# Linear attention into a phase-mixing MLP on one core: first q's by Pool's casting fetches, key-value products in runs of two, and a re-planned order

## The chip, the cores and the metric

The kernel runs on one core of a Trainium2 chip. The metric is the device time of the whole program in microseconds (us), here the median of several runs. The engines are PE (TensorE, the matrix array), DVE (VectorE), ACT (ScalarE), POOL (GpSimd) and SP (SyncE, which here only issues transfers).

## What is computed

Eight batches (B), eight heads (H), 576 positions (S), 64 columns a head (D); C = H·D = 512. Everything comes in and goes out as float32.

```python
kv  = einsum('bhsd,bhse->bhde', k, v)
out = einsum('bhsd,bhde->bhse', q, kv)
x   = out / sqrt(mean(out**2, -1) + 1e-6) * g_norm      # then heads side by side: [8, 576, 512]
theta = x @ w_theta
y   = w_tok_r @ (x * cos(theta)) + w_tok_i @ (x * sin(theta))   # over positions
u   = x + y
result = u + maximum(u @ w_ch, 0)
```

## The kernel before

A batch's 576 positions are worked on as four full tiles of 128 rows and a tail of 64. The functions inside the main function each describe one step of one batch `b`, and pair of heads `hp` or row tile `ti`:

- `load` (L402): q, k and v of a pair of heads, 256 or 288 KB each, fetched by SP. With `b < Q_SOFT`, q is fetched by Pool instead, as fp16 (L409), after a one-word copy of an earlier v tile on Pool (`hold`, L382, L385) that keeps Pool from running ahead. The tails of 64 rows are small fetches of their own; from batch 2 on, q's tail is fetched by Pool (L457). `hold` also keeps back the token mixers (L511, L516, until v number `MIX_AFTER`) and the channel weights (L544).
- `cast_q` (L598): DVE turns q into fp16 (L600). With `b < Q_SOFT` only the tail is cast (L606).
- `turn_q_pair` (L769): PE turns q of a pair, four 128-wide matmuls (L783), or with `b < Q_SOFT` eight, one for each head and row tile, into halves of the array's columns (L778); ACT or DVE copies the result into qT (L794, L796). `turn_q_tail` (L910) does the tail, and `double` (L744) copies its columns a second time so that the tail uses 128 columns. From batch 4 on, q is turned by a DMA (L626, L632).
- `attention` (L643): kv products in float32, in half of the array (L662); `KV_RUN` pairs stand in one task from batch 2 on. In batches 0 and 1 `by_pair` (L803) goes on pair by pair: raw product (L823), square (ACT, L830), sum (DVE, L836), root, scale (xp, L860), turn (xTps, L871), copy (xT, L882 and L884). Later batches do this by row tile in `norm` (L691) and `turn_x` (L934), where Pool takes the root (L721).
- `phase` (L986): theta product (PE, L996, L1001), its folding (pt on ACT, f and fa on DVE), two sines (tr on ACT, L1031, L1039), and z = x times both (DVE, L1049).
- `mix` (L1071): the token mixing y (PE, L1092), in six parts a batch; parts 0 and 1 of batch 0 are opened early and fed row tile by row tile. DVE forms uT (L1103).
- `channel` (L1125): u turned back by PE (ups, L1141) and copied by ACT (L1157), or, for batches from `U_FROM` up to the last, turned by a DMA (L1179); the product with w_ch (vps, L1150); the result (ot, DVE, L1161); its store.
- `idle_work` (L390): filler matmuls on PE that read nothing new (tile warm, L395).

None of these runs where it stands. Each is handed to `Weave.add` (L134) with the engines that could do it, a cost, a due time, the tasks that it needs and the buffers that it makes and uses. `Weave.run` (L145) then plans the order: it starts each engine at a time in `BEGIN`, keeps its own account of engines, transfers and buffers (`SLOTS`, L44), and on the engine that can begin first takes the task with the earliest due time. Due times are `START + PERIOD * b + first + every * i` from the table `DUE` (L21). `MARGIN`, `SLACK`, `URGENT`, `AHEAD` and `HOLD` shift its choices; `HOLD` is added where a task would change the array's form (whole array, halves, quarters). A filler is taken where PE has nothing else that can begin as early, up to the planned time `WARM`. The planned order is then fixed on each engine (`in_traced_order`, L246): on the chip every engine works through its list in that order, and waits at the head of it. The lists are thus known before the program runs, and both kernels' can be compared.

```python
def due(stage, b, i):
    (first, every) = DUE.get((stage, b), DUE[stage])
    return START + PERIOD * b + first + every * i
```

Of the kernel before, what the change touches and what calls it, by code (L numbers as in the profile page):

```python
# [15 lines left out]

PERIOD = 26.95
START = 4.0  # L20
DUE = {  # L21
    "load": (-21.61, 8.44),
    "theta": (0.39, 0),
    "mixers": (17.6, 0),
    "wch": (24.7, 1.25),
    "wT": (21.7, 1.67),
    ("phase", 0): (19.67, 0),
    ("mix", 0): (28.68, 4.96),
    ("channel", 0): (31.53, 7.53),
    ("phase", 1): (11.06, 3.64),  # L30
    ("mix", 1): (31.68, 5.24),
    ("channel", 1): (50.99, 7.88),
    ("first", 1): (-24.56, 1.26),
    "first": (0.46, 0),
    "cast": (27.66, 0.92),
    "turn_q": (-15.49, 0.49),
    "attention": (-2.51, 1.53),
    "norm": (-1.15, 4.11),
    "turn": (4.17, 1.73),
    "phase": (18.31, 3.76),  # L40
    "mix": (51.46, 2.87),
    "channel": (75.2, 4.3),
}
SLOTS = {  # L44
    "kv": 1, "raw": 2, "tp": 2, "th": 1, "mm": 3,
# [4 lines left out]
BANK = {"th": "mm", "y": "mm", "vp": "mm", "pu": "tp", "px": "tp"}  # L50
QUAD = 2
Q_DMA = 4
U_FROM = 2
X_FROM = 8
MIX_AFTER = 2
WCH_AFTER = 8
KV_RUN = 1
Q_SOFT = 0
QL_SOFT = 1


# [44 lines left out]
class Weave:  # L106
# [5 lines left out]

    SLACK = {"PE": 0.2, "ACT": 0.004, "DVE": 0.078, "POOL": 0.1, "SP": 0.05}
    MARGIN = {"PE": 0.247, "ACT": 0.026, "DVE": 0.555, "POOL": 0.1, "SP": 0.0}
    BEGIN = {"PE": 1.6, "ACT": 3.2, "DVE": 1.7, "POOL": 2.5, "SP": 0.73}
    WARM = 69.7
    COLD = 5.0
    URGENT = 5.5  # L120
    AHEAD = 0.3
    HOLD = 2.45
    DRAIN = 0.095
    ENTRY = {"F": 0.011, "R": 0.011, "H": 0.024, "K": 0.048, "Q": 0.048}
    ARRAY = {"F": 0, "R": 1, "H": 2, "K": 2, "Q": 3}
# [19 lines left out]
    def run(self):  # L145
# [25 lines left out]
        while ready:  # L171
            best = {}
            for t in ready:
# [8 lines left out]
                for (e, cost, lat, port) in engines:  # L182
                    new = e == "PE" and self.ARRAY[port] != form
                    clear = free[e] + self.DRAIN if new else free[e]
                    start = max(clear, at + self.MARGIN[e], port_free if port is True else 0.0)
                    if name[0] == "warm" and start > self.WARM:
                        continue
                    if due < self.URGENT:
                        start = max(clear, start - self.AHEAD)
                    best.setdefault(e, []).append(  # L190
                        (start, due + self.HOLD * new, max(at, port_free) if port is True else at, t, cost, lat, port)
                    )
            picks = []
            for (e, c) in best.items():
                first = min(x[0] for x in c) + self.SLACK[e]
                (start, due, at, t, cost, lat, port) = min(
# [66 lines left out]
def kernel(  # L263
# [45 lines left out]
    def sb(kind, shape, dtype, name):  # L309
        return work.tile(shape, dtype, tag=kind, bufs=SLOTS[kind], name=name)  # L310
# [53 lines left out]
    def dve(cost, fast=False):  # L364
        return ("DVE", cost, cost + 0.14, fast)

    def pe(cost, form="F"):
        return ("PE", cost, cost + 0.22, form)
# [13 lines left out]
    def hold(name, due, after):  # L382
        def fn(e):
            t = st[after]
            nc.gpsimd.tensor_copy(late[:], t[:, 0, 0:1] if len(t.shape) == 3 else t[:, 0, 0, 0:1])  # L385
        weave.add(name, [("POOL", 0.2, 0.22, False)], due, fn, needs=[after],
                  uses=["{}{}_{}".format(*after)])
# [14 lines left out]
    def load(b, hp):  # L402
        pair = slice(2 * hp, 2 * hp + 2)

        def part(kind, src):
            def fn(e):
                if kind == "q" and b < Q_SOFT:
                    t = sb("qh", [P, 2, NF, D], FP16, f"q{b}_{hp}")
                    nc.gpsimd.dma_start(  # L409
                        out=t[:].rearrange("p h j d -> p h (j d)"),  # L410
                        in_=src[b, pair, 0:SF, :].rearrange("h (p j) d -> p h (j d)", j=NF),
                    )
                elif kind == "q" or b >= QUAD:
                    t = sb(kind, [P, 2, NF, D], FP32, f"{kind}{b}_{hp}")
                    nc.sync.dma_start(
                        out=t[:].rearrange("p h j d -> p h (j d)"),
                        in_=src[b, pair, 0:SF, :].rearrange("h (p j) d -> p h (j d)", j=NF),
                    )
                else:
                    t = sb(kind, [P, NS, D], FP32, f"{kind}{b}_{hp}")  # L420
                    nc.sync.dma_start(
                        out=t[:].rearrange("p j d -> p (j d)"),
                        in_=src[b, pair].rearrange("h (p j) d -> (h p) (j d)", j=NS),
                    )
                st[kind, b, hp] = t
# [14 lines left out]
        for (i, (kind, src)) in enumerate((("q", q), ("k", k), ("v", v))):  # L440
            full = kind == "q" or b >= QUAD
            if kind == "q" and b < Q_SOFT:
                n = b * HP + hp
# [26 lines left out]
    def load_weights():  # L470
# [36 lines left out]
        use = due("mixers", 0, 0)  # L507
        hold("hold_mix", use, ("v", MIX_AFTER // HP, MIX_AFTER % HP))
        for (i, w) in enumerate((moe_w_tok_r, moe_w_tok_i)):
# [88 lines left out]
    def cast_q(b, hp):  # L598
# [8 lines left out]

        if hp == 0 and b < Q_SOFT:
            weave.add(("qcl", b), [dve(0.33, True)], due("first", b, hp) + (0.1 if b else 9.0), tail,
                      needs=[("ql", b)], makes=[("qc", f"qc{b}")], uses=[f"ql{b}"])  # L610
        if b < Q_SOFT:
            return
# [30 lines left out]
    def attention(b, hp):  # L643
        run = KV_RUN if b >= QUAD and b > 1 else 1

# [123 lines left out]
    def turn_q_pair(b, hp, at):  # L769
# [3 lines left out]
        def turn_q0(e):  # L773
            t = st[pq] = ps("tp", [P, SF], FP16, pq)
            for j in range(NF):
                if b < Q_SOFT:
                    for r in range(2):
# [10 lines left out]
        def keep_q0(e):  # L788
# [6 lines left out]
            else:  # L795
                nc.vector.tensor_copy(t, src)  # L796

        weave.add((pq,), [pe(0.226, "H" if b < Q_SOFT else "F")], at, turn_q0, needs=[("qc" if b >= Q_SOFT else "q", b, hp)], makes=[("tp", pq)],
                  uses=[f"qc{b}" if b >= Q_SOFT else f"q{b}_{hp}"])
# [325 lines left out]
    def channel(b, ti):  # L1125
# [5 lines left out]

        pu_on = not U_FROM <= b < B - 1 or ti == NF

# [71 lines left out]
# [4 lines that stand above are left out]
# [59 lines left out]
```

## Time and profile before

| | us |
|---|---|
| median of 3 runs | 214.65 (214.16 to 215.4) |
| the profiled execution | 215.4 |
| its span, first to last instruction | 213.6 |
| PE / DVE / ACT / POOL busy in the span | 203.7 / 177.3 / 150.5 / 89.6 |
| filler matmuls on PE (50) | 11.2 |
| y products (PE, L1092) | 78.1 |
| float32 kv products (PE, L662), k and v without tails | 27.1 |
| q casts on DVE (L600), 32 | 13.2 |
| theta product of batch 0 begins | 21.62 |

A timeline line gives the start, the duration, engine, source line, operation, output<-input with sizes, the number of instructions merged into it, and in brackets the idle time before it with what ended it. Matmuls overlap each other, so a matmul's own duration is longer than the step from one to the next, and a busy PE is not PE at its peak; where PE's work is counted here, it is by the step from start to start. A line of stretches gives the stretch and its length, then for PE, its weight loads, DVE, ACT and POOL the busy time with the number of instructions, the granted TensorE clock, the busy share of the DMA engines, and GB/s.

### The profile page before, as it was taken

To read this page: it belongs to the slowest core of one execution; us is meant where nothing else is said; L and a number is where in the kernel's file an instruction comes from. 1 tells how busy PE (TensorE), PEld (TensorE's weight loads), DVE (VectorE), ACT (ScalarE), POOL (GpSimd) and SP (SyncE) were. 2 spreads that over 40 slices of the span, in tenths; PEclk is the share of its full clock that TensorE was granted. 3 is DMA by queue.
4 is the path that set the end of the run, shared out by engine and by line. 5 is a ranking of instruction groups with operands and counts; after the bars stand their busy time and mean duration, and the time that the engine had idled before them with its cause. 6 is when DMAs were issued, how large, how long until landed. Compare 5 with 4: busy or idle time off the path is not lost.

```text
span 213.6 us, 5833 instructions
## 1 busy us (share of the span) xinstructions
PE 203.7 (95%) x2305; PEld 145.0 (68%) x2305; DVE 177.3 (83%) x355; ACT 150.5 (70%) x294; POOL 89.6 (42%) x104
## 2 busy tenths in 40 slices
PE   6897989999999999999999999999999999999992
PEld 4784567876488777677787577765777467568560
DVE  3178689877978889999999998999999989973652
ACT  2077699967984899898897859789688588550031
POOL 8050106595105763575474436574474733000000
PEclk9999999999999999999999999999999999999998
DMA  6999999999587599989898989859773263344424
GB/s 182 371 360 247 264 373 282 374 213 209 97 268 238 146 284 356 211 254 230 242 179 154 324 304 189 158 136 330 229 166 79 79 170 75 135 114 98 146 103 172
DMA packets 62463, 45.62 MB, mean 214 GB/s; under 512 B 33380, under 2 KB 55524, under 8 KB 62436
## 3 DMA queue, kind: packets, MB, share of 16 engines
q1 hardware_dynamic: 58272, 43.01, 70.7%
q0 software_dynamic: 4160, 2.25, 8.4%
q8 instruction: 18, 0.29, 0.6%
q14 instruction: 9, 0.07, 0.2%
q10 hardware_dynamic: 4, 0.00, 0.0%
HBM read 33.06 MB, written 9.44 MB: 199 GB/s over the span
## 4 chain that ended last, share of the span: by engine, by line
PE 62%; DVE 11%; DMA 8%; ACT 8%; POOL 6%; issue 2%; SPq 0%; DVEq 0%
PE y L1092 25%; PE vps L1150 12%; PE th L996 9%; PE kv L662 7%; DMA wch<-in_moe_w_ch_dram 4%; POOL rt L721 3%; DMA v<-in_v_dram 3%; PE xTps L943 2%; PE raw L699 2%; DVE ss L710 2%; POOL rt1h L855 2%; ACT tr L1031 2%; DMA k<-in_k_dram 2%; PE ups L1141 2%; DVE x L733 2%
## 5 line engine op out<-in xcount | busy, mean ns | idle before, releaser
L1092 PE MATMUL y<-wT,z 128*128 128x320 f16 (+1 forms) x576 | 78.1, 286 | 0.1
L1092 PEld LDWEIGHTS <-z 128*128 128x128 f16 x576 | 55.0, 98 | 16.2 <-issue 0.6
L721 POOL TENSOR_TENSOR rt<-ss,mhalf 128x8 f32<-128x8 f32 x31 | 56.5, 1822 | 2.6
L1150 PE MATMUL vps<-wch,uT 128*128 128x512 f16 (+1 forms) x192 | 36.5, 344 | 0.3 <-DMA wch<-in_moe_w_ch_dram 0.2
L1103 DVE SCALAR_TENSOR_TENSOR uT<-y,gcol,xT 128x320 f16<-128x320 f32 (+1 forms) x48 | 29.3, 613 | 6.9 <-PE y L1092 6.9
L1008 ACT ACTIVATE pt<-th,magic_t 128x512 f32<-128x512 f32 (+1 forms) x40 | 25.8, 645 | 9.1 <-PE th L996 5.6
L996 PE MATMUL th<-wth,xT 128*128 128x512 f16 x128 | 32.0, 379 | 0.0
L717 POOL TENSOR_SCALAR ss<-ss 128x8 f32<-128x8 f32 x31 | 8.4, 272 | 55.6 <-DVE ss L710 54.8
L662 PE MATMUL kv<-v,k 128*64 128x64 f32 (+1 forms) x672 | 27.1, 232 | 0.9 <-DMA v<-in_v_dram 0.9
L662 PEld LDWEIGHTS kv<-v,k 128*64 128x64 f32 (+1 forms) x672 | 24.3, 145 | 4.7 <-issue 3.6
L1012 DVE SCALAR_TENSOR_TENSOR f<-pt,th 128x512 f32<-128x512 f32 (+1 forms) x40 | 25.1, 628 | 2.5 <-ACT pt L1008 2.4
L1031 ACT ACTIVATE tr<-fa,pio_t 128x512 f16<-128x512 f32 x32 | 23.0, 720 | 1.8 <-DVE fa L1019 1.6
L1031 ACT ACTIVATE tr<-f 128x512 f16<-128x512 f32 x32 | 20.2, 630 | 5.6 <-DVE f L1012 5.4
L952 ACT ACTIVATE xT<-xTps,gcol 128x512 f16<-128x512 f16 (+1 forms) x32 | 20.1, 629 | 5.2 <-PE xTps L943 5.0
L733 DVE TENSOR_TENSOR x<-raw,rt 128x512 f16<-128x512 f32 x32 | 22.0, 686 | 2.1 <-POOL rt L721 1.6
L710 DVE TENSOR_REDUCE ss<-sq 128x8 f32<-128x512 f32 x32 | 21.8, 680 | 2.0 <-ACT sq L706 2.0
L1150 PEld LDWEIGHTS <-uT 128*128 128x128 f16 (+1 forms) x192 | 14.7, 102 | 11.7 <-issue 1.1
L1157 ACT COPY u<-ups 128x512 f16<-128x512 f16 (+1 forms) x20 | 9.9, 500 | 16.7 <-PE ups L1141 16.7
L1049 DVE TENSOR_TENSOR z<-x,tr 128x1024 f16<-128x1024 f16 (+1 forms) x32 | 19.7, 618 | 1.3 <-ACT tr L1039 0.9
L706 ACT ACTIVATE sq<-raw 128x512 f32<-128x512 f32 x32 | 19.0, 593 | 0.5 <-PE raw L699 0.5
L600 DVE CAST qcast<-q 128x512 f16<-128x512 f32 x32 | 13.2, 422 | 6.2 <-DMA q<-in_q_dram 6.2
L996 PEld LDWEIGHTS <-xT 128*128 128x128 f16 x128 | 11.5, 98 | 10.1 <-ACT xT L952 0.2
(105 smaller groups left out, 264.0 us busy)
## 6 DMA issues: line engine op xcount, KB each, us to landing
q<-in_q_dram SPq DMA_DIRECT2D x32, 256.0 KB, 5.0
out_dram<-ot SPq DMA_DIRECT2D x32, 256.0 KB, 3.0
k<-in_k_dram SPq DMA_DIRECT2D x24, 256.0 KB, 5.1
v<-in_v_dram SPq DMA_DIRECT2D x24, 256.0 KB, 4.9
k<-in_k_dram SPq DMA_DIRECT2D x8, 288.0 KB, 5.6
v<-in_v_dram SPq DMA_DIRECT2D x8, 288.0 KB, 5.5
wst<-in_moe_w_theta_dram SPq DMA_DIRECT2D x4, 256.0 KB, 5.8
out_dram<-ot SPq DMA_DIRECT2D x16, 64.0 KB, 2.1
```

Of the source, the lines that this page charges most:

```text
L662: nc.tensor.matmul(kvp[r * D:(r + 1) * D, hp, :], kt, vt, start=(j == 0), stop=(j == (NT if b >= QUAD else NS) - 1),)
L710: nc.vector.reduce_sum(out=t[:], in_=st[sq][:].rearrange("p (h e) -> p h e", h=H), axis=mybir.AxisListType.X,)
L721: nc.gpsimd.tensor_tensor(out=r[:], in0=t[:], in1=mhalf[:], op=ALU.pow)
L733: nc.vector.tensor_tensor(out=t[:].rearrange("p (h e) -> p h e", h=H), in0=st[raw][:].rearrange("p (h e) -> p h e", h=H), in1=st[rt][:].un ...
L952: nc.scalar.activation(out=st["xT", b][:, :, cols], in_=st[px][:, :, 0:cols.stop - cols.start], func=AFT.Copy, scale=gcol[:],)
L996: nc.tensor.matmul(t[:], xT[:, kc, :], wth[:, kc, :], start=(kc == 0), stop=(kc == NK - 1),)
L1008: nc.scalar.activation(out=t[:], in_=st[th][:], func=AFT.Identity, bias=magic_t[:])
L1012: nc.vector.scalar_tensor_tensor(out=t[:], in0=st[pt][:], scalar=MAGIC, in1=st[th][:], op0=ALU.subtract, op1=ALU.subtract,)
L1031: nc.scalar.activation(out=t[:, which, :], in_=src[:], func=AFT.Sin, scale=-RAD, bias=0.0 if bias is None else bias[:],)
L1092: nc.tensor.matmul(st[y][:, c, :], z[:, kc * P:(kc + 1) * P], wT[m][:, cols], start=(c == 0 and m == 0) if open_sums else m == 0, stop=m = ...
L1103: nc.vector.scalar_tensor_tensor(out=st["uT", b][:, chunks, cols], in0=st[y][:], scalar=gcol[:], in1=st["xT", b][:, chunks, cols], op0=ALU ...
L1150: nc.tensor.matmul(t[half], uT(kc), wch[:, kc, r * n:(r + 1) * n], start=(kc == 0), stop=(kc == NK - 1),)
```

## The change

Only constants change; the functions stay as they are.

- `Q_SOFT` 0 to 2: q of batches 0 and 1 is fetched as fp16 by Pool and turned per head in column halves; its cast on DVE goes (8 of 32).
- `KV_RUN` 1 to 2: from batch 2 on, the kv products of two pairs are one task.
- `U_FROM` 2 to 3: u of batch 2 is turned by PE and copied by ACT, not turned by DMAs.
- `MIX_AFTER` 2 to 4: the token mixers' fetch is held for the first v of batch 1, not for the third of batch 0.
- The due times, the period and the planner's margins change, and with them the order on every engine.

Counted in the fixed lists: fillers 50 to 63; turns of u on PE (L1141) 80 to 96; turns of q in halves 0 to 64, whole ones (L783) 64 to 32; u copies on ACT 20 to 24; Pool's one-word copies 2 to 7. Of the four weight casts of wth ACT does one, not three, and DVE three; DVE also takes over three doublings of q's tail, two more qT copies, two more kv copies, one more xT and one more tail copy from ACT; ACT takes over two of the copies of the token mixers (wT).

In the new order SP begins with k and v of batch 0, then k and v of batch 1's first pair, the q tail of batch 1 and the weights of theta. Pool begins, after its memsets, with q of pairs 0 and 1, and puts a one-word copy before each later q. PE does kv of pair 0, both first turns of q, kv of pair 1, and then the first raw product; the first kv product, two turns of q and the first raw product of batch 1 come before the theta product of batch 0, as do 30 fillers in a row right ahead of it.

```diff
-PERIOD = 26.95
+PERIOD = 26.25
 START = 4.0
 DUE = {
-    "load": (-21.61, 8.44),
-    "theta": (0.39, 0),
-    "mixers": (17.6, 0),
-    "wch": (24.7, 1.25),
-    "wT": (21.7, 1.67),
-    ("phase", 0): (19.67, 0),
-    ("mix", 0): (28.68, 4.96),
-    ("channel", 0): (31.53, 7.53),
-    ("phase", 1): (11.06, 3.64),
-    ("mix", 1): (31.68, 5.24),
-    ("channel", 1): (50.99, 7.88),
-    ("first", 1): (-24.56, 1.26),
-    "first": (0.46, 0),
-    "cast": (27.66, 0.92),
-    "turn_q": (-15.49, 0.49),
-    "attention": (-2.51, 1.53),
-    "norm": (-1.15, 4.11),
-    "turn": (4.17, 1.73),
-    "phase": (18.31, 3.76),
-    "mix": (51.46, 2.87),
-    "channel": (75.2, 4.3),
+    "load": (-20.73, 8.57),
+    "theta": (0.3, 0.18),
+    "mixers": (5, 2.14),
+    "wch": (26.18, 0),
+    "wT": (19.93, 1.64),
+    ("phase", 0): (19.83, 0),
+    ("mix", 0): (27.65, 4.99),
+    ("channel", 0): (30.95, 7.53),
+    ("phase", 1): (11.16, 3.64),
+    ("mix", 1): (31.19, 5.47),
+    ("channel", 1): (54.0, 9.88),
+    ("first", 1): (-21.76, 2.05),
+    "first": (-10.54, 0.2),
+    "cast": (20.69, 3.24),
+    "turn_q": (-15.49, 0.67),
+    "attention": (-2.25, 1.53),
+    "norm": (-0.36, 4.34),
+    "turn": (-0.42, 1.23),
+    "phase": (18.31, 3.54),
+    "mix": (52.55, 4.01),
+    "channel": (69.29, 7.16),
 }
...
-U_FROM = 2
+U_FROM = 3
 X_FROM = 8
-MIX_AFTER = 2
+MIX_AFTER = 4
 WCH_AFTER = 8
-KV_RUN = 1
-Q_SOFT = 0
+KV_RUN = 2
+Q_SOFT = 2
 QL_SOFT = 1
...
-    SLACK = {"PE": 0.2, "ACT": 0.004, "DVE": 0.078, "POOL": 0.1, "SP": 0.05}
-    MARGIN = {"PE": 0.247, "ACT": 0.026, "DVE": 0.555, "POOL": 0.1, "SP": 0.0}
+    SLACK = {"PE": 0.141, "ACT": 0.06, "DVE": 0.084, "POOL": 0.1, "SP": 0.05}
+    MARGIN = {"PE": 0.179, "ACT": 0.168, "DVE": 0.402, "POOL": 0.1, "SP": 0.0}
     BEGIN = {"PE": 1.6, "ACT": 3.2, "DVE": 1.7, "POOL": 2.5, "SP": 0.73}
-    WARM = 69.7
+    WARM = 72.0
     COLD = 5.0
-    URGENT = 5.5
-    AHEAD = 0.3
-    HOLD = 2.45
+    URGENT = 5.1
+    AHEAD = 0.24
+    HOLD = 4.61
```

## The prediction

> **What bounds the kernel now.** I read the page's busy shares first, then the stretches of the span, then the stretches of the filler matmuls alone, and last the timelines of single engines in the first 45 us. The page:
>
> ```profile
> PE 203.7 (95%) x2305; PEld 145.0 (68%) x2305; DVE 177.3 (83%) x355; ACT 150.5 (70%) x294; POOL 89.6 (42%) x104
> ```
>
> The stretches (PE, weight loads, DVE, ACT, POOL, granted clock, DMA share, GB/s):
>
> ```profile
> 7.20:21.60 14.40, 13.07 (x210) 10.61 (x211) 9.46 (x23) 7.74 (x21) 2.81 (x5) 1.00 1.07 325
> 21.60:44.60 23.00, 21.70 (x324) 16.40 (x323) 18.02 (x42) 20.48 (x44) 8.86 (x11) 1.00 1.07 327
> 44.60:90.00 45.40, 45.15 (x565) 32.31 (x563) 40.43 (x79) 37.13 (x73) 22.51 (x24) 1.00 0.92 217
> 90.00:170.00 80.00, 79.66 (x874) 56.67 (x873) 77.74 (x150) 65.98 (x125) 45.53 (x46) 1.00 0.82 205
> ```
>
> The same stretches for the tile warm alone, that is, filler:
>
> ```profile
> 7.20:21.60 14.40, 3.94 (x22) 0.00 (x0) 0.00 (x0) 1.00 1.07 325
> 21.60:44.60 23.00, 3.44 (x14) 0.00 (x0) 0.20 (x1) 1.00 1.07 327
> 44.60:90.00 45.40, 0.28 (x1) 0.00 (x0) 0.00 (x0) 1.00 0.92 217
> ```
>
> The reader is to see two regimes. From 44.6 us on PE is full with real work: 45.15 of 45.40, then 79.66 of 80.00, with one filler matmul. There the end moves only with the amount of PE work. Before 44.6 PE is kept busy with filler, DMA is saturated (share 1.07), and from 21.6 on ACT (20.48 of 23.00) and DVE (18.02) carry the path. So the question is when PE reaches the full regime: the first product of batch 0 that comes after the opened sums, y0_2, starts at 44.58 (the eleven matmuls at 44.36 are the last two of y0_1, 0.11 each, and nine of y0_2). What follows until the last matmul at 209.5 is a packed stream.
>
> PE around the first theta product, and Pool at the start:
>
> ```profile
> 18.68 1.68 PE L395 MATMUL warm<-kvbd 128*128 128x256 f16 x10
> 20.73 0.40 PE L871 MATMUL xTps0h<-ident,xp 128*128 128x128 f16 x4 [0.38 <-DVE xp L860]
> 20.97 0.82 PE L395 MATMUL warm<-kvbd 128*128 128x256 f16 x6
> 21.62 2.75 PE L996 MATMUL th<-wth,xT 128*128 128x512 f16 x12
> ```
> ```profile
> 4.42 1.09 POOL L355 MEMSET wnatl<- 64x576 f16 x2
> 5.46 0.20 POOL L356 MEMSET wtt<- 64x128 f16 x1
> 11.51 0.19 POOL L385 COPY late<-v 128x1 f32<-128x1 f32 x1 [5.84 <-DMA v<-in_v_dram]
> 12.04 0.79 POOL L511 DMA_DIRECT2D wnat<-in_moe_w_tok_r_dram  x1 [0.35 <-issue]
> ```
>
> Pool clears tiles until 5.66; today nobody waits for that. Six fillers stand ahead of the theta product, at (21.62-20.97)/6 = 0.11 us each.
>
> **The change part by part, in the order of the path.** Both instruction orders are fixed when the kernel is built, so I count in them.
>
> *First q.* Today q of pair 0 is SP's first fetch (issued 0.72, cast by DVE at 3.55, so 2.8 us). Changed, it is Pool's first fetch, behind the same memsets: issue at 5.66. The trace has no 256 KB fetch by Pool. The nearest rows are Pool's 64 KB q tails: 2.8 us to landing on a quiet DMA, 5.9 in the median. I take 3.6, nearer the quiet end, since nothing is ahead of it in Pool's queue: q0_0 lands at 9.3. The next three follow in one queue; at 381 GB/s (5 to 14 us) 262 KB take 0.7 us alone and 1.4 beside SP's fetches, which I take: q0_1 at 10.7, q0_3 at 13.5. Bounds: 2.8 and 0.7 give 9.2 for q0_1; 5.9 and 2.1 (a third of the rate) give 13.7 for q0_1 and 17.9 for q0_3.
>
> *Waits that are added on Pool.* Before q0_2 and each later q Pool copies a word of a v tile, so it waits for SP's fetches, v0_0 onwards; those land from 7.1 on today and earlier without q between them, so Pool passes as it gets there. Behind these waits stand the token mixers' fetches, held for v1_0, SP's tenth fetch, instead of v0_2, its ninth. Issued near 13 instead of 12.04, with 8.6 and 11.4 to land, they are there at 22 to 25; the first turn of them is now behind th0_3, after 28. Covered; without that cover it would cost the 1 us.
>
> The Trainium skill ("DMA: Bandwidth & Descriptors", section Anatomy of one DMA) fits a Pool fetch as 2.0 us plus bytes over 436 GB/s. By it, as an estimate, q0_0 would land at 8.3.
>
> *First raw product.* In the changed order PE runs kv0_0, both turns of q0_0 and q0_1, then kv0_1, and only then raw0h0; it waits in order. From q0_1: 0.2 to react, 0.28 turn, kv0_1 1.4 (a pair takes 1.2 at 35.67, and two took 4.2 at 7.24), raw 0.22 and 0.2, square 0.60 and 0.2: the first sum of squares on DVE at 13.8, against 12.99 today: +0.8 (bounds -0.7 and +3.8).
>
> *From there to the last turn of x in batch 0.* DVE took 12.99 to 20.68, nearly without a gap. Out of this chain go a cast (0.43), a qT copy (0.42) and a weight cast (0.38); in come a scaled copy of xT (0.48), a kv copy (0.44) and the cast of batch 1's q tail (0.41). Nothing is gained: the turn moves from 20.73 to 21.5. The other three casts that go stood before 12.99, where DVE was idle (2.4 us before the cast at 7.82 alone).
>
> *Filler.* The changed order has 30 warm matmuls between that turn and th0_0, not 6. They wait for no data, but PE must run them: 24 x 0.11 = 2.6. th0_0: 21.62 + 0.8 + 2.6 = 25.0. In all there are 63 fillers, not 50.
>
> *th0_0 to y0_2*, 22.96 today. From the first f to the last z of batch 0 DVE loses four q casts (1.7), two wT copies (0.9) and an xp (0.7), and gains a kv copy, the doubled tail and its copy (1.1): -2.2. ACT loses about 2.2 from the first sine to the last (two qT copies and a tail copy, a kv copy, an xT; it gains a square), but its sine starts later after th0_0: qTpl0 now stands behind all four theta products and xTps1h0, +1.1 us, and two wT copies and a square of batch 1 now come before it, 0.5 each by start to start, less two copies that go: +0.6. The first sine at 29.66 is 8.0 after th0_0; that becomes 9.7. ACT alone gives -0.5, DVE alone -2.2. I take -1.2, nearer ACT, which is the fuller engine (20.48 of 23). y0_2 is then 0.8 + 2.6 - 1.2 = 2.2 late.
>
> *After y0_2.* Batch 2's u goes through PE again: 16 turns, 4 x 0.22 = +0.9; four u copies on ACT (0.59 each) lie in a stretch where ACT has 15.3 of 20; four transposes leave SP's queue, which had 1.3 each for issuing. kv in runs of two: visits of PE to half-array work fall from 21 to 19. A visit costs 0.05 to enter, 0.10 before and 0.10 after (78.02 to 79.65): -0.5. Little, because the old order already ran most pairs together. A turn of x and raw1_4 are done before y0_2 in the new order: -0.4. Batch 1 is also 1.3 us further on DVE and ACT at that point; DVE has 77.74 of 80.00 afterwards, so I give that -0.2. The turning of q in halves: eight half-width matmuls where four were; the nearest row, four of 128*64 in 0.14, makes 0.28 of 0.22, eight times +0.06 = 0.5 (0 to 1.8 if halves don't overlap), nearly all before y0_2 in PE's waiting time. If that cover is gone it is 0.5.
>
> Sum: +2.2 + 0.9 - 0.5 - 0.4 - 0.2 = **+2.0 us**. The profiled execution took 215.4 (span 213.6, 1.8 around it) and is the slowest of three; the change is added to the median: 214.65 + 2.0 = **216.6 us** (217.4 against the profiled one).
>
> A row and a rule that speak against the change: Pool issues at 45.12 took 1.52 for two while DVE was busy for 12.49 of 15 us, so no issue was held for long. The Trainium skill ("SBUF — State Buffer", section SBUF: two separate sides) says that a DVE copy in a two-port mode locks Pool out of writing descriptors. By it each of the eight new issues could wait for one copy (0.42 to 0.46 by rows), 3.6 us in all on Pool; but DVE is idle at the first four.
>
> **Rivals.**
> *Relief wins (faster).* DVE loses 8 casts, and the stretch 21.6 to 44.6 is ACT's and DVE's. With q at its early bound (-0.7), the fillers (+2.6) and DVE's full -2.2, y0_2 starts 0.3 early; then +0.9 - 0.5 - 0.4, and the relief takes the pauses of PE after 44.6 with it (about 0.4 at 54, 0.6 at 93 to 96, 0.5 at 166 to 168: -1.5): -1.8, 212.8 us. It decides if y0_2 starts before 44.3. For it: ACT's 20.48 of 23. Against: the fillers run in any case.
> *Both cancel.* q at the early bound with my other terms: +0.5; or the full relief with my q: +1.0. About 215.4.
> *Pool's queue starves.* q0_1 at 13.7 instead of 10.7: +3 more, 219.6. For it: the 5.9 us median at DMA share 1.07. Against: SP's queue has less to do at that time.
> *The change doesn't do what it says*: runs of two hardly change the visits (21 to 19); that is in the sum.
>
> **How the numbers follow.** Forecast 0.40, starved queue 0.10, cancel 0.20, relief 0.30. Within 0.5% (1.07 us, about what a measurement of this kernel can tell from no change) is 213.6 to 215.7. The first two are slower, 0.50; cancel is the same, 0.20; relief is faster, 0.30. The range takes in relief and most of the starved case: 212.2 to 219.0. The forecast's own range is 215.7 to 218.0.
>
> **What would show it.** Right: the first q landing after 9, th0_0 at 24 to 26, y0_2 at 46 to 47.5, then PE full with one filler, and 16 more turns of u. Wrong: th0_0 before 23, or y0_2 before 44.6; or PE pausing after y0_2 for a k or v fetch, or for DVE, which the sum has nowhere.

## The result and the profile after

The changed kernel takes 221.59 us (median of 4 runs, 220.88 to 222.03), the kernel before 214.47 beside it (214.16 to 215.4): a ratio of 1.032, 95% interval 1.028 to 1.037. It is 7.1 us slower; 2.0 were forecast, and 219.0 was the end of the range. The profiled execution took 222.03, its span 220.3, against 215.4 and 213.6.

The page of the changed kernel, its busy shares and the granted clock in 40 slices:

```profile
PE 205.6 (93%) x2366; PEld 146.7 (67%) x2366; DVE 177.3 (80%) x358; ACT 148.6 (67%) x286; POOL 92.5 (42%) x119
...
PEclk9857999999999999999999999999999999999999
```

The stretches, in the columns of before (PE, weight loads, DVE, ACT, POOL, granted clock, DMA share, GB/s):

```profile
7.20:21.60 14.40, 8.15 (x128) 6.50 (x130) 4.14 (x9) 3.33 (x11) 6.69 (x15) 0.64 1.18 276
21.60:44.60 23.00, 21.83 (x348) 16.20 (x345) 17.96 (x44) 15.53 (x32) 7.96 (x13) 1.00 0.97 270
...
90.00:170.00 80.00, 79.81 (x940) 57.53 (x938) 76.88 (x150) 67.75 (x129) 43.48 (x46) 1.00 0.99 226
```

The second of them for filler alone (PE, DVE, ACT, clock, DMA share, GB/s), 43 matmuls where 14 were:

```profile
21.60:44.60 23.00, 6.69 (x43) 0.00 (x0) 0.20 (x1) 1.00 0.97 270
```

The first stretch is where it went: PE was busy for 13.07 of 14.40 us before, now for 8.15, and even DVE fell from 9.46 to 4.14. PE, DVE and ACT mostly wait, and the clock is at 0.64. From 90 us on PE is as full as before. Pool's issue of the first two q's, and PE's own timeline, from the first product to theta:

```profile
5.34 1.68 POOL L409 DMA_DIRECT2D q<-in_q_dram  x2
```
```profile
5.53 1.26 PE L662 MATMUL kv<-v,k 64*64 64x64 f32 x36
12.68 0.64 PE L778 MATMUL qTps0h<-ident,q 128*64 128x128 f16 x8 [5.89 <-DMA q<-in_q_dram]
...
14.46 2.19 PE L662 MATMUL kv<-v,k 64*64 64x64 f32 x36
16.57 0.61 PE L823 MATMUL raw0h<-kvbd,qT 128*128 128x128 f16 x4
...
27.48 3.44 PE L395 MATMUL warm<-kvbd 128*128 128x256 f16 x30
30.76 1.04 PE L996 MATMUL th<-wth,xT 128*128 128x512 f16 x4
31.72 0.40 PE L871 MATMUL xTps1h<-ident,xp 128*128 128x128 f16 x4
```

The first q, issued at 5.34, lands at 12.64, 7.30 us later; PE waits 5.89 us for it (a line's idle time is in its brackets). The same 36 matmuls of a kv product take 1.26 us before the pause and 2.19 after it. In numbers that add up to the span (before, after, difference):

| | before | after | |
|---|---|---|---|
| first raw product starts | 11.94 | 16.57 | +4.63 |
| from there to the last turn of x, xTps0h3 | 8.79 | 10.69 | +1.90 |
| from there to th0_0 | 0.89 | 3.50 | +2.61 |
| from th0_0 to y0_2 | 22.96 | 21.70 | -1.26 |
| from y0_2 to the last product with w_ch | 164.33 | 162.87 | -1.46 |
| from there to the end of the span | 4.7 | 4.9 | +0.2 |

So 9.1 us are lost before th0_0 and 2.7 come back after it.

### The profile page after: what moved, and what is told of

It is laid out like the page before. It is cut to its first block, busy times and chain, and to the rows that moved or that the text cites. A ratio compares the mean times of both kernels' runs of the same rounds, so it can differ in the third digit from the quotient of the medians.

```text
span 220.3 us, 5981 instructions
## 1 busy us (share of the span) xinstructions
PE 205.6 (93%) x2366; PEld 146.7 (67%) x2366; DVE 177.3 (80%) x358; ACT 148.6 (67%) x286; POOL 92.5 (42%) x119
## 4 chain that ended last, share of the span: by engine, by line
PE 82%; ACT 8%; DMA 3%; POOL 2%; DVE 1%; issue 1%; DVEq 0%; POOLq 0%
PE y L1092 31%; PE vps L1150 13%; PE th L996 13%; PE kv L662 9%; DMA q<-in_q_dram 3%; PE raw L699 3%; PE xTps L943 3%; PE ups L1141 2%; PE warm L395 2%; ACT tr L1031 2%; PE th L1001 2%; ACT tr L1039 2%; ACT wT L587 1%; PE raw0h L823 1%; ACT sq1h L830 1%
## 5 line engine op out<-in xcount | busy, mean ns | idle before, releaser
L721 POOL TENSOR_TENSOR rt<-ss,mhalf 128x8 f32<-128x8 f32 x31 | 53.1, 1713 | 2.6
L1150 PE MATMUL vps<-wch,uT 128*128 128x512 f16 (+1 forms) x192 | 37.1, 344 | 0.0
L662 PE MATMUL kv<-v,k 128*64 128x64 f32 (+1 forms) x672 | 26.2, 229 | 0.0
L662 PEld LDWEIGHTS kv<-v,k 128*64 128x64 f32 (+1 forms) x672 | 23.6, 143 | 3.3 <-issue 2.8
L1157 ACT COPY u<-ups 128x512 f16<-128x512 f16 (+1 forms) x24 | 12.3, 518 | 17.4 <-PE ups L1141 17.4
L1150 PEld LDWEIGHTS <-uT 128*128 128x128 f16 (+1 forms) x192 | 14.4, 102 | 10.1 <-issue 0.6
L1161 DVE SCALAR_TENSOR_TENSOR ot<-vps,u 128x512 f32<-128x512 f32 (+1 forms) x24 | 14.4, 599 | 2.6 <-PE vps L1150 2.5
```

What stands on the lines that cost most here:

```text
L662: nc.tensor.matmul(kvp[r * D:(r + 1) * D, hp, :], kt, vt, start=(j == 0), stop=(j == (NT if b >= QUAD else NS) - 1),)
L721: nc.gpsimd.tensor_tensor(out=r[:], in0=t[:], in1=mhalf[:], op=ALU.pow)
L1150: nc.tensor.matmul(t[half], uT(kc), wch[:, kc, r * n:(r + 1) * n], start=(kc == 0), stop=(kc == NK - 1),)
```

## The experiments

Theory A: the first q's come late, because Pool clears tiles first and then because the fetch itself takes 7.3 us. Theory B: PE's pause for them halves the speed of the matmuls behind it. Theory C: the 30 fillers delay theta. The rivals stand in each expectation. Where nothing else is said, the planned order of the changed kernel is kept and only the lines shown are edited. Later theories (P: DVE waits for Pool's root; S: the fetch shares the DMA; T: the small tail of q) came from these runs.

### e1: clearing on DVE

```diff
-        nc.gpsimd.memset(t[T:P, NF], 0.0)        # qcast; likewise kl, vl, wnatl, wtt
+        nc.vector.memset(t[T:P, NF], 0.0)
```

> The changed kernel, with Pool's clearing of the tails (qcast, kl, vl, wnatl, wtt) done by DVE, which is idle then; the order of everything else stays. Pool can then issue the first q near 1.4 us, not at 5.34. Theory A (the loss is the late first q: late issue and slow fetch, with PE waiting in order behind it): the first q lands 3 to 4 us earlier (8.5 to 9.5), th0_0 starts at 26.5 to 28 instead of 30.76, and the time falls by 3 to 4 us, to 217.5 to 218.5. Rival D (the fetches share a full DMA, so an earlier issue lands hardly earlier because SP's k and v go first): the first q lands after 11, and the time falls by less than 1 us, 220.6 or more.

Measured: 219.19 us, ratio to before 1.018 (1.012 to 1.024), 2.4 us better than the changed kernel. The first q is issued at 1.43 and lands at 8.57, th0_0 starts at 27.43, both as A said; the time falls by less than its 3 to 4. Pool and PE of e1:

```profile
1.43 1.69 POOL L409 DMA_DIRECT2D q<-in_q_dram  x2
```
```profile
10.86 0.41 PE L778 MATMUL qTps0h<-ident,q 128*64 128x128 f16 x8 [1.82 <-DMA q<-in_q_dram]
11.20 2.13 PE L662 MATMUL kv<-v,k 64*64 64x64 f32 x36
```

An issue 3.91 us earlier lands 4.07 earlier: the clearing that nobody waited for before is on the path now. But issue to landing is 7.14 us again, and the kv product behind the pause of 1.82 still takes 2.13; the granted clock from 11.2 to 14.4 is 0.52.

### e2: fillers in the pause

```diff
                 times(i)
+            if b == 0 and hp == 0:
+                t = ps("mm", [P, SH], FP32, "bridge")
+                for i in range(48):
+                    nc.tensor.matmul(...)        # as in idle_work
```

> The changed kernel, with 48 more filler matmuls right after the first pair's k times v, so that PE does not pause for 5.9 us before the first turn of q. Nothing else moves. Theory B (the pause lowers TensorE's clock, and the products until about 20 us run at half speed): the second pair's k times v takes 1.2 to 1.4 us instead of 2.19, the granted clock in 7.2 to 21.6 is over 0.9 instead of 0.64, th0_0 starts 1.5 to 2.5 us earlier, and the time falls to 219 to 220. Theory A alone (only the landing of q counts, the rest waits on DVE and ACT): th0_0 and the time stay within 0.5 us, 221 to 222.

Measured: 220.33 us, ratio 1.024 (1.018 to 1.031); 1.3 us better than the changed kernel.

```profile
7.70 5.66 PE L654 MATMUL bridge<-kvbd 128*128 128x256 f16 x48
...
14.18 1.26 PE L669 MATMUL kv<-v,k 64*64 64x64 f32 x36
```

B holds: the same kv product takes 1.26 and not 2.19, th0_0 starts at 29.17, 1.59 earlier. The gain in time is somewhat below the forecast 1.6; the 48 fillers end 0.6 us after q is there, which may be why. The ranges of the two kernels' runs overlap (219.99 to 221.56 and 220.88 to 222.03), so it is the trace that carries this. The first kv product takes 2.19 in this profile, and 1.26 in that of the changed kernel, where PE's list is the same up to there: the half speed of PE's first microseconds ends at one time in one execution and later in another. The comparison above is of the second product.

### e3: no fillers ahead of theta

```diff
+            if 23 <= n < 53:
+                return
             t = ps("mm", [P, SH], FP32, name)
```

> The changed kernel without the 30 filler matmuls that stand right ahead of th0_0; the order of everything else stays. Theory C (the fillers are on the path in full): th0_0 starts up to 3.3 us earlier but not before the weights and xT are there, 28.4 to 29.1, so 1.7 to 2.3 us earlier, and the time falls by as much, to 219.3 to 220. Rival (DVE and ACT set y0_2, the fillers only fill their lead): th0_0 earlier, y0_2 within 0.5 us of 52.46, time 221 to 222.

Measured: 223.57 us, ratio 1.038 (1.031 to 1.044). That is 2.0 us slower than the changed kernel. Neither C nor its rival said so.

```profile
27.61 0.82 PE L998 MATMUL th<-wth,xT 128*128 128x512 f16 x2
...
31.86 0.40 PE L873 MATMUL xTps1h<-ident,xp 128*128 128x128 f16 x4 [2.16 <-DVE xp L862]
32.09 4.34 PE L998 MATMUL th<-wth,xT 128*128 128x512 f16 x12
```
```profile
31.11 0.69 DVE L862 TENSOR_TENSOR xp<-raw1h,rt1h 128x512 f16<-128x512 f32 x1 [1.84 <-POOL rt1h L857]
...
32.70 0.68 DVE L1014 SCALAR_TENSOR_TENSOR f<-pt,th 128x512 f32<-128x512 f32 x1
```

th0_0 does start 3.15 us earlier. But batch 1's first pair has been put ahead of theta's other tiles: PE stands before xTps1h0 until DVE has xp of that pair, and DVE waits 1.84 us for its root from Pool. xTps1h0 starts at 31.86 here and at 31.72 with the fillers. The fillers only filled this wait; and without them PE pauses 2.16 us, and the twelve theta matmuls behind it take 4.34 us instead of 2.75. The Trainium skill ("TensorE: Matmul & The Clock Gate", Part 1: The HAM clock gate) says that the array runs at half its clock by default and after an idle window of about 3.4 us, and at full clock after about as much steady work. The halving agrees. The window does not: here half speed followed pauses of 1.82 (e1) and 2.16 us, while full speed followed one of 1.55 us (e5 below). Behind the pause of 2.16 the granted clock is 0.71; over the products around the first turns of q it reads 1.00, though the kv product at 14.43 took 2.19: there only the durations show it. The stretches behind the pause and of those products:

```profile
31.00:36.00 5.00, 4.14 (x16) 1.76 (x17) 3.03 (x6) 1.38 (x2) 1.91 (x6) 0.71 1.04 349
12.00:16.00 4.00, 2.77 (x46) 2.37 (x48) 0.85 (x2) 0.00 (x0) 2.76 (x7) 1.00 1.23 280
```

### e4: e1 and e2 together

e1 with `root_d` (which the first small product reads) cleared first, 14 fillers after the first kv product and 18 after the first turn of q.

```diff
+                for i in range(14):              # after kv0_0; 18 more after qTps0h0
+                    nc.tensor.matmul(...)
```

> The changed kernel with Pool's clearing of tails done by DVE (as in e1, but with the one-element tile root_d, which the first small product reads, cleared ahead of them), 14 filler matmuls after the first pair's k times v and 18 after the first turn of q, so that PE has no pause before the first raw product. If the late first q and the low clock are two separate losses, their gains add: 2.4 (e1) and 1.3 (e2), a time of 217.5 to 218.2, with the first raw product near 12.3 and th0_0 near 26. If the clock was already cured by the shorter pause of e1, the time stays at 219.

Measured: 218.57 us, ratio 1.018 (1.011 to 1.026); 3.0 better than the changed kernel, where a plain sum gives 3.7; against e1 alone, 0.6 better, the ranges overlap. All kv products take 1.26, the first raw product starts at 12.77, th0_0 at 26.26. With the head as early as this, 4.1 us to the kernel before are left.

### e5: q by SP

```diff
-Q_SOFT = 2
+Q_SOFT = 0
```

The order is planned anew.

> The changed kernel with Q_SOFT 0 and all else as changed (due times, runs of two, batch 2's u on PE, mixers held for v number 4); the order is planned anew. Theory A (the loss is the first q's by Pool): the first raw product is back at 12 to 13, th0_0 at 22 to 25, and the time at 212.5 to 216. Rival E (the new due times and the rest cost as much whichever way q comes): 219 or more.

Measured: 217.54 us, ratio 1.013 (1.008 to 1.017). That lies between A's range and E's. q by Pool, with what the new plan makes of it, thus costs 4.0 us of the 7.1, and 3.1 stay. The first raw product is at 10.94, earlier than before; the first sine comes at 32.48, and 29.66 before. DVE of e5:

```profile
24.20 0.69 DVE L860 TENSOR_TENSOR xp<-raw1h,rt1h 128x512 f16<-128x512 f32 x1 [1.89 <-POOL rt1h L855]
...
26.95 0.42 DVE L606 CAST qcast<-ql 64x512 f16<-64x512 f32 x1 [1.46 <-DMA ql<-in_q_dram]
```

Two waits in DVE's list, ahead of the first folding of theta and right behind it: Pool's root for batch 1 as in e3, and the small q tail of batch 0, which is fetched after batch 1's into the one buffer there is for both. PE pauses 1.55 us behind the second wait, and the four theta matmuls that follow still run at full speed:

```profile
27.42 0.29 PE L916 MATMUL qTpl<-ident,qcast 128*128 128x64 f16 x4 [1.55 <-DVE qcast L606]
27.55 1.03 PE L996 MATMUL th<-wth,xT 128*128 128x512 f16 x4
```

### e6, e9, e10: one part in the plan of before

The kernel before with `Q_SOFT` 2 (e6), with all four switches (e9), and with the three others without `Q_SOFT` (e10); due times and planner constants are those of before.

```diff
-Q_SOFT = 0
+Q_SOFT = 2        # e6
...
-KV_RUN = 1
+KV_RUN = 2        # e10, with U_FROM = 3 and MIX_AFTER = 4; e9 has all four
```

> The kernel before with Q_SOFT 2 and nothing else changed; the order is planned anew. Theory A (q by Pool costs about 4 us wherever it is put, as between e5 and the changed kernel): 217.5 to 219.5, the first raw product after 16. Rival (it costs only together with the new due times): 216 or less.

> The kernel before with all four switches of the change (Q_SOFT 2, KV_RUN 2, U_FROM 3, MIX_AFTER 4) but with its own due times and planner constants. e5 showed that without q by Pool 2.8 us stay. Theory F (these 2.8 come from the new due times): the time is that of Q_SOFT alone, 217.5 to 219.5. Rival G (they come from runs of two, batch 2's u on PE or the later mixers): 220.5 or more.

> The kernel before with KV_RUN 2, U_FROM 3 and MIX_AFTER 4, q still by SP, and its own due times; the order is planned anew. If these parts are what makes the changed kernel 1.5 us shorter after y0_2, the time is 213 to 214 and that stretch as short as the changed one's, 162.9 from y0_2 to the last matmul. If the gain belongs to the new due times: within 0.5 us of the kernel before or slower.

Measured: e6 227.43 us (ratio 1.060, 1.053 to 1.068), e9 229.73 (1.072, 1.062 to 1.081), e10 228.20 (1.062, 1.058 to 1.067). The ranges named for them are missed by some 8 us and more; the open ends of two rivals take the times in, but not for their reasons. In e6 the first raw product starts at 17.40, as A said, but more is lost behind it. In e10 q comes early (first raw product 10.74), and the plan falls into this wait, among others:

```profile
29.55 0.42 DVE L606 CAST qcast<-ql 64x512 f16<-64x512 f32 x1 [5.61 <-DMA ql<-in_q_dram]
```

DVE stands 5.61 us before the cast of a small tail, with all that is behind it in its list. I read such a run as measuring how badly the due times of one plan fit another set of switches, not what a switch costs. What runs of two, batch 2's u on PE and the later mixers are worth by themselves stays open.

### e12 and e17: SP held back

e12 is e1 (with `root_d` first) where SP's third fetch waits for Pool's first q; e17 is e13 (below) where SP's fifth waits for the second q, with fewer bridge fillers.

```diff
+                    if (kind, b, hp) == ("k", 0, 1):           # e17: ("k", 0, 2) and q0_1
+                        nc.vector.tensor_copy(t[:, 0, 0:1], w[:, 0, 0, 0:1])   # w: q0_0, fetched just before
```

> As e1 (Pool's clearing on DVE, root_d first), and SP's third fetch (k of the second pair) waits until Pool's first q has landed, because DVE first copies one word of that q into its tile. Only k and v of pair 0 then run beside the first q. Theory S (the 7.3 us from issue to landing is time in a shared, full DMA): q lands 3 to 4.5 us after its issue, by 4.5 to 6. Rival L (Pool's casting fetch of this form needs about 7 us by itself): it lands at 8 or later, as in e1 (8.57 from an issue at 1.43). The time is no aim here, since k and v come later.

> e13 with SP's fifth fetch (k of the third pair) waiting until Pool's second q has landed, because DVE first copies one word of that q into its tile, and fewer bridge fillers (4 and 8). Theory S (what is left of the late q is the sharing of the DMA with SP's k and v): q of pairs 0 and 1 land by 6.5 and 8.5, the first raw product starts at 9.5 to 10.5 instead of 13.54, and the time falls by 2.5 to 3.5 us, to 214 to 215.2. Rival K (k and v of the later pairs, or the weights of theta behind them, then come as much later): y0_2 within 1 us of e13's 47.31, time 216.5 to 218.5.

Measured in e12 (one run, 222.19 us): the first q, issued at 1.42, lands at 5.76, 4.34 us later instead of 7.14; the third, issued at 4.45 while SP's next fetch is not issued before 5.97, at 7.87, 3.42 later. S holds, L falls. Of the 2.8 us between e1's 7.14 and these 4.34, 0.8 lie before q's first packet and 2.0 behind it. The DMA queues (packets, MB, share of 16 engines; q1 is SP's, q0 Pool's), in the changed kernel from 6 to 9.3 us, then from 9.5 to 11, and in e12 from 4 to 5.5:

```profile
DMA packets 605, 1.24 MB, mean 375 GB/s; under 512 B 68, under 2 KB 68, under 8 KB 605
...
q1 hardware_dynamic: 605, 1.24, 101.9%
```
```profile
q1 hardware_dynamic: 182, 0.36, 69.8%
q0 software_dynamic: 200, 0.10, 49.4%
```
```profile
DMA packets 419, 0.20 MB, mean 134 GB/s; under 512 B 26, under 2 KB 419, under 8 KB 419
...
q0 software_dynamic: 419, 0.20, 109.7%
```

In the changed kernel Pool's q, issued at 5.34, moves no packet until 9.38, while SP's have the engines. Then both queues move about as many packets, 182 and 200, but SP's carry 2304 bytes and Pool's 512: SP gets 0.36 MB and q 0.10 of them; in e1 from 5 to 8 us it is 337 and 326 packets, 0.71 and 0.15 MB. The Trainium skill ("DMA: Bandwidth & Descriptors", section Queues, rings and completion order) says that a DMA engine takes turns between its queues packet by packet; the counts agree. They say nothing of the 4 us in which Pool's queue moves no packet at all.

e17 is 221.03 us (ratio 1.032, 1.027 to 1.037): K was right in direction, and it is worse than K's 216.5 to 218.5. The three first q's land at 8.66, 9.21 and 9.88, behind k and v of pair 1, the first raw product starts at 12.16 instead of e13's 13.54; but v of pair 2 lands at 13.96, and Pool's fetches for batch 1, which wait for SP's v tiles, at 21.61 and 22.93: PE waits 1.11 and 0.58 for them, and y0_2 is at 50.12. Holding SP's queue back as a whole does not pay here.

### e13 and e18: the root by ACT and DVE, half the fillers

e18 is the changed kernel with these two edits, e13 is e4 with them.

```diff
         def power(e):
+            if (b, hp) == (1, 0):
+                root(e)
+                invert(e)
+                return
...
+            if 38 <= n < 53:
+                return
             t = ps("mm", [P, SH], FP32, name)
```

> e4 with two more edits: the root of batch 1's first pair (rt1h0) is taken by ACT and DVE as in batch 0, not by Pool's power, and 15 of the 30 fillers ahead of th0_0 go. Theory P (the folding of theta waits in DVE's order for xp of batch 1's first pair, and that waits 1.84 us for Pool; the fillers only fill this wait, which is why e3 lost): th0_0 near 24.7 instead of 26.26, the first folding of theta (f) near 26 instead of 28.06, the time 216 to 217. Rival T (the first sine waits for batch 0's tail anyway, whose q lands near 29): the time stays within 0.7 us of e4, 217.9 to 219.2.

> The changed kernel with only the two edits by which e13 differs from e4: the root of batch 1's first pair by ACT and DVE, and 15 of the 30 fillers ahead of th0_0 gone. Theory P: from the first raw product to y0_2 1.8 us less (34.1 instead of 35.9), time 219.6 to 220.3. Rival: these two edits helped only because q came earlier in e13 (in the changed kernel q of batch 1 and the weights land late as well): time within 0.6 us of 221.6.

Measured: e18 220.16 us (ratio 1.026, 1.021 to 1.031), 1.4 better than the changed kernel; from the first raw product to y0_2 33.87 us instead of 35.89. e13 217.59 (1.015, 1.008 to 1.022), 1.0 better than e4, the same stretch 33.77 instead of 35.61. In e13 the first q landed 0.77 us later than in e4, which may hide part of the gain; its time lies between P's range and T's, and its runs overlap e4's. P holds in e18, in time and trace, and in e13 in the trace. The root alone, with all 30 fillers kept, was not run. DVE of e18:

```profile
27.98 0.20 DVE L849 RECIPROCAL rt1h<-ss1h 128x8 f32<-128x8 f32 x1 [0.37 <-ACT ss1h L845]
...
28.73 0.68 DVE L866 TENSOR_TENSOR xp<-raw1h,rt1h 128x512 f16<-128x512 f32 x1
...
30.31 0.68 DVE L1018 SCALAR_TENSOR_TENSOR f<-pt,th 128x512 f32<-128x512 f32 x1
```

The wait of 1.84 us is gone, and the first folding of theta starts at 30.31 instead of 32.56.

### e14 and e15: batch 0's tail first

```diff
-due("load", b, hp) + (0.04 if b else 1.15)
+due("load", b, hp) + (2.0 if b == 1 else 0.04 if b else 0.55)
```

In e5 (e14) and in the changed kernel (e15); planned anew.

> e5 (q by SP, all else as changed) with q's tail of batch 0 fetched ahead of batch 1's: only the due times of these two small fetches are edited; the order is planned anew, and the tail's raw product moves ahead of th0_0. Theory T (in e5 the first sine starts 2.8 us later than before, 32.48 against 29.66, because batch 0's tail is fetched second and lands at 26.9): the first sine is back at 29.5 to 30.5 and the time at 214 to 215.5. Rival P (the fillers and batch 1's first pair ahead of theta hold it): the first sine after 31.5, the time 216.5 or more.

> The changed kernel with q's tail of batch 0 fetched ahead of batch 1's, as in e14; the order is planned anew. Theory T: the first sine, 40.40 in the changed kernel, comes 1.5 to 2.5 us earlier, and the time falls to 219 to 220.2. Rival P: first sine within 0.7 us, time 221 to 222.

Measured: e14 221.11 us (ratio 1.030, 1.024 to 1.035), e15 221.82 (1.033, 1.029 to 1.038). T falls: in e15 the first sine comes at 32.89 instead of 40.40, y0_2 only 2.1 earlier, and the time is that of the changed kernel. In e14 the first sine comes at 30.04, as T said, and the time does not follow: the wait has only moved to the other tail:

```profile
29.56 0.28 PE L916 MATMUL qTpl<-ident,qcast 128*128 128x64 f16 x4 [3.45 <-DVE qcast L606]
30.06 1.87 PE L996 MATMUL th<-wth,xT 128*128 128x512 f16 x4 [0.23 <-DVE f L1012]
```

PE waits 3.45 us for batch 1's tail, and four theta matmuls then take 1.87 instead of 1.04.

### e16: the three waits out of e5

e5's order, with the root as in e18, 8 of 20 fillers gone, and two buffers for the small tail.

```diff
-                    t = sb("ql", [T, H, D], FP32, f"ql{b}")
+                    t = work.tile([T, H, D], FP32, tag="ql", bufs=2, name=f"ql{b}")
```

> e5 (q by SP, all else as changed, its order kept) with three edits that take out what holds theta there: the root of batch 1's first pair by ACT and DVE, not Pool (DVE waited 1.89 us for it), 8 of the 20 fillers ahead of th0_0 gone, and a second buffer for the small q tail, so that batch 0's is fetched at once and not only after batch 1's has been cast (DVE waited 1.46 us for it). Theory P with the tail: the 2.8 us that e5 loses against the kernel before go, th0_0 near 22, y0_2 near 44.6, time 213.8 to 215.2. Rival R (the remaining loss lies in batch 1's first work standing ahead of batch 0's, not in these waits): 216 to 217.5.

Measured: 214.92 us, ratio 1.001 (0.997 to 1.005): the kernel before is reached again, 2.6 us are back. Batch 0's tail lands at 20.03 instead of 26.93. With q by SP the rest of the change costs and brings nothing that can be told within 0.5%, once these waits are gone; so the order's own part of the 7.1 us was in them. Which of the three edits brings how much was not separated.

### e19 and e20: no pause in the head

12 fillers, in e16 (e19) and in the kernel before (e20).

```diff
+                for i in range(10):              # ahead of kv0_0; 2 more ahead of qTps0h0
+                    nc.tensor.matmul(...)
```

> e16 with 2 fillers ahead of the first turn of q and 10 ahead of the first k times v, so that PE has no pause in its first 7 us. Theory B (a pause costs the matmuls their full speed for some 4 us after it; in e16 the first two k times v take 2.1 us each, not 1.26): the two take 1.26 to 1.5 each, the first raw product starts 0.8 to 1.2 us earlier, and the time falls by 0.5 to 1 us, to 213.9 to 214.4. Rival (v of pair 1 lands when it lands, or the 12 fillers themselves run at half speed and delay the first): no change or up to 1 us more.

> The kernel before with the same 12 fillers in the same places. Theory B: the first two k times v, 4.19 us together at half speed, take 2.5 to 3, the first raw product starts 0.5 to 1 us before 11.94, and the time falls by up to 0.8 us, to 213.8 to 214.6. Rival: as for e19, no change or up to 1 us more.

Measured: e19 215.27 us (ratio 1.003, 1.000 to 1.006), e20 214.47 (0.997, 0.994 to 1.000). PE of e20, both first products in one line:

```profile
7.67 2.31 PE L669 MATMUL kv<-v,k 64*64 64x64 f32 x72
```

And PE of the kernel before:

```profile
1.49 2.32 PE L395 MATMUL warm<-kvbd 128*128 128x256 f16 x10 [1.49 <-DVE root_d L348]
...
5.13 1.25 PE L395 MATMUL warm<-kvbd 128*128 128x256 f16 x5
7.24 4.19 PE L662 MATMUL kv<-v,k 64*64 64x64 f32 x72 [0.86 <-DMA v<-in_v_dram]
...
11.94 0.38 PE L823 MATMUL raw0h<-kvbd,qT 128*128 128x128 f16 x4 [0.18 <-ACT kvbd L816]
```

In the profile the fillers do what B said: the first two kv products take 2.31 us together, and 4.19 in the kernel before, and y0_2 starts at 43.13 instead of 44.58. But in the kernel before the fillers ahead of them run at half speed too (ten in 2.32 us, and 0.11 each ahead of theta), so PE had not been at full speed before its pause of 0.86: steady work brings it there sooner, and the pause alone is not shown to be the cause. The medians show less: e19 gains nothing, and e20, with the lowest ratio of this study, is at most 0.6% faster than before, with an interval that just reaches no change.

## Why the prediction was wrong, step by step

The sign was right, and the failed step is *first q*, with the step *first raw product* that was built on it. In the profiles y0_2 is 7.9 us late, not 2.2: of the 5.7 between, 4.3 had come by the first sum of squares and 1.4 more by the last turn of x.

*First q.* The issue was at 5.34, near my 5.66, but q0_0 took 7.30 us from issue to landing, not 3.6: q0_0, q0_1 and q0_3 landed at 12.64, 13.85 and 17.13, where I had 9.3, 10.7 and 13.5. The reason that I gave for the row near the quiet end, that nothing is ahead of q in Pool's queue, was the mistake: the engines are shared with SP's queue, and my own window showed them at a share of 1.07. On a quieter DMA the fetch does take 3.42 to 4.34 us (e12). The upper row, 5.9, was the nearer one, and still too low against 7.30. The fit that I quoted from the Trainium skill ("DMA: Bandwidth & Descriptors", section Anatomy of one DMA) gave 8.3 as an estimate, still earlier than my 9.3; the measured 12.64 decides.

*First raw product.* +0.8 was forecast, with +3.8 as the far end; the first sum of squares on DVE came at 18.13, +5.14. The raw product itself is 4.63 late. Of this the late issue is about 3.3 (e1: 13.27), and the half speed behind the pause 1.2 (e2: 15.38). The late issue itself was in my sum. What was not is 3.15 us of q0_1's landing, and 1.2 in the steps from there to the sum of squares, which took 4.28 and not 3.1: I took kv0_1 at 1.4, and it took 2.11 to the next task. That early products can run at half speed was readable in the kernel before, whose first two kv products took 4.19 us; I noted them and took the faster row.

*Waits on Pool.* Nearly as forecast: the mixers' fetches were issued at 13.66 and 14.76 and took 9.0 and 11.0 us. The trace has eight of Pool's one-word copies, six of them ahead of a q; the count of seven above is one short.

*From there to the last turn of x.* "Nothing is gained" was too kind: 10.69 us instead of 8.79. e4, with the clock up throughout, still has 9.99, so some 0.7 is the clock; the other 1.2 I put down to the order, which puts work of batch 1 between, without a run that shows it.

*Filler.* The arithmetic was right: 3.50 between the last turn and th0_0, and 0.89 before, so +2.61 against 2.6. The meaning was wrong. The fillers stand in a wait for Pool's root of batch 1's first pair, behind which theta is queued on DVE and PE. Without them the kernel is slower (e3); with the root elsewhere and half of them it is 1.4 us faster (e18). th0_0 comes as much later as I said, and the end does not hang on it. That Pool takes the root (L855) for batch 1's pairs too, and who waits for it, was nowhere in my sum.

*th0_0 to y0_2.* -1.2 forecast, -1.26 measured; the first sine 9.64 after th0_0 where 9.7 was forecast. But e15 shows that this sine could come 7.5 us earlier for little, so the number came out right by luck, without the sine being what decides.

*After y0_2.* -0.2 forecast, -1.46 measured. The relief that I gave 0.2 is the likelier cause, since the pauses of PE that I listed at 54, 93 to 96 and 166 to 168 are gone and only one over 0.15 us is left (0.19, before theta at 97.12, for ACT's xT); it is argued, not shown, since no run undoes one part of this stretch alone.

*The rivals.* The starved queue, at a chance of 0.10, had the landings almost exactly (13.7 and 17.9, measured 13.85 and 17.13), and its 219.6 was 2.0 too low; the clock (e2: 1.3) and Pool's root with the fillers (e18: 1.4) had no place in it. The relief did come after y0_2 (its -1.5 of pauses), while its condition, y0_2 before 44.3, was missed by 8 us. The rule on the shared port is not tested in the head: DVE is idle from 4.20 to 13.36 in the changed kernel, while Pool issues six q's.

*What would show it.* q after 9: yes. th0_0 at 24 to 26, y0_2 at 46 to 47.5: no, 30.76 and 52.46. PE without pauses for DVE or fetches after y0_2: yes.

*What the 7.1 us are.* By the medians: 4.0 for q by Pool (e5, planned anew), of which the order of Pool's clearing is 2.4 (e1), the pause's effect on PE 1.3 (e2), together 3.0 (e4); 2.6 for the waits that the new order puts ahead of theta (e16 against e5), of which the root and the fillers are 1.4 in the changed kernel (e18). The two sums come from different plans and need not add exactly.

## What to carry to other kernels

Price a moved transfer by the busiest stretch in which it will run, not by its own queue: here two queues shared the DMA engines packet by packet, and the one with the small packets got the fewer bytes. Whoever moves the first load of a kernel to another engine must look at what stands ahead of it on that engine, and add to the wait itself what a pause of TensorE costs the matmuls behind it. A row of fillers in an in-order list can mark a wait: ask what the next instruction is waiting for before counting the fillers as its price.

## What was not expected of the hardware

- Matmuls at half speed behind pauses of 1.82 us (e1: a kv product of 2.13 instead of 1.26, clock 0.52) and 2.16 us (e3: twelve theta matmuls in 4.34 instead of 2.75, clock 0.71), and not behind one of 1.55 us (e5). The clock column can read 1.00 over products at half speed: e3 from 12 to 16 us, and the kernel before from 7.20 to 21.60, with its kv products of 4.19 us.
- A casting fetch fills the DMA engines at a third of the rate of a plain one, in bytes written: 134 GB/s at a share of 109.7% in 512-byte packets (e12), against 375 GB/s at 101.9% in packets of mostly 2304 bytes (the changed kernel, 6 to 9.3 us). By these rates, as an estimate, 131 KB of fp16 q take 0.98 us of all engines, and 262 KB of float32 q 0.70. The packets of q themselves say the same: SP's of float32 q, 1024 bytes each, take 47 ns in the mean (the kernel before, 5 to 14 us), and Pool's of the same q as fp16, 512 bytes each, 66 ns (e12, 4 to 5.5 us). The cast halves the bytes and saves the DMA nothing.
- The time from Pool's issue to the first packet is 4.0 us in the changed kernel (5.34 to 9.38), 3.0 in e1 (1.43 to 4.40) and 2.2 in e12 (1.42 to 3.58). Why the start too depends on what else runs was not tried.
